# Attention, experts and MLP in one kernel: idle matmuls, a q load and the steps of batches 1 to 3's attention are put elsewhere

## The chip, the cores and the metric

One Trainium2 chip, one of its cores. The metric is the device time of one execution in microseconds (us), as the median of three runs. TensorE is called PE here, VectorE DVE, ScalarE ACT, GpSimd POOL, and SyncE, which issues the loads, SP; those are the profile's own names.

## What is computed

Three stages follow each other. Attention is done twice per batch and head: 32 packed rows `p` attend to `k` and `v`, and then the queries `q` attend to the 32 packed results. Four experts and an MLP work on the result.

```
def sm_attn(qq, kk, vv):
    s = scale * np.matmul(qq, kk.transpose(0, 1, 3, 2))
    a = np.exp(s - np.max(s, axis=-1, keepdims=True))
    a = a / (np.sum(a, axis=-1, keepdims=True) + 1e-09)
    return np.matmul(a, vv)
p_packed = sm_attn(p, k, v)                 # 4 batches, 8 heads, 576 tokens, 64 wide
out = sm_attn(q, p_packed, p_packed)
x = out as 2304 rows of 512
x = sum over 4 experts e of probs[:, e] * (relu(x @ w1[e]) @ w2[e])     # 512 -> 1024 -> 512
r = relu(x @ w_in);  out = (s * r * r + b) @ w_out                      # 512 -> 2048 -> 512
```

## The kernel before

All instructions of one engine run in the order in which the program writes them, and that order is written by hand. Batch 0's attention comes first, as straight code. Then a long loop runs over units: one unit is one expert, one batch, one half of its tokens and one block of 128 hidden columns, 16 units for each expert and batch. In step `i` the loop first runs the pieces that are woven in at that step (`run(i)`, filled by `at(step, function, ...)`), then the first product `m1` of unit `i+2` (6 matmuls of 288 columns, L693), then the second product `m2` of unit `i` (12 matmuls, L721). Each `m1` result goes through ACT (`hh`, L703) and DVE (`hl`, L704). `at_fin` makes the attention result `a2` of a batch, which `m1` of that batch reads. After the last block of a half, DVE takes the four accumulators away into `x2` (L745).

The attention of batches 1 to 3 is woven into these steps, piece by piece. For batch `n` the pieces are numbered from a step `s0`, and a table lists (offset, function, half). The pieces that matter here are, with the names of their tiles:

- `trans_kq`: DVE turns k or q in blocks of 32 (`kT`, `qT`, L148). Two buffers of each half serve both, so the `kT` of the next batch follows on the `qT` of this one.
- `at_s1`: PE multiplies p with k for one half of the tokens (`s1`, 16 matmuls, L187). It needs both `kT` tiles.
- `at_max1`: DVE takes the row maximum (`m2`, L199). For the first half of batches 1 to 3, ACT also copies the scores to SBUF (`a1`, L201), since their PSUM banks are wanted again.
- `at_exp1`: DVE makes the negative maximum `nm` (L208); ACT takes the exponentials of both halves (L219), of the first half from the copy in SBUF, of the second from PSUM.
- `at_a1t`: PE turns the exponentials (`tr`, four matmuls L230 into one bank, one L235 into another), ACT copies them out.
- `at_pv`, `at_pn`, `at_pt`: the product with v (L248), its normalisation by DVE or ACT (`pw`, then `sbd`), and its transposition (L287) with a copy by ACT (`ptw`, L288).
- `at_s2` to `at_fin`: q times the packed rows (L299), softmax over 32 columns on DVE, POOL and ACT (L311 to L339), and `a2` as a high and a low part (L358, L359).

The PSUM banks of tag `m` are two. `s1`, `tr`, `pv`, `pt` and `s2` of batches 1 to 3 and the products `fold_w1` take them in turn, so a matmul that opens a bank waits until whoever read the bank's last content is done. `expert_weights` (L946) is a piece of step 3: four DVE instructions on the gate probabilities and a store.

SP issues the loads in program order, and a load can be issued only when the one eight before it has landed. PE begins with 11 matmuls on a tile of zeros (`warm`, L922), before data is there. Step numbers in the prediction are those of the loop; batch 1 starts at step `s0` = 2, batch 2 at 16, batch 3 at 32.

Of the kernel before, what the change touches and what calls it, by code (L numbers as in the profile page):

```python
# [11 lines left out]
AF = mybir.ActivationFunctionType  # L12
# [7 lines left out]
def attention_experts_mlp_kernel(  # L20
# [87 lines left out]
    def load_k(bi, gi, cuts=None):  # L108
        if ("k", bi, gi) not in kq_in:
            kq_in["k", bi, gi] = att.tile([P, NJ * D], F32, tag="kq", bufs=4, name=f"k{bi}{gi}")  # L110
        x = k_src[bi, 4 * gi : 4 * gi + 4].rearrange("h (r j) d -> (h r) (j d)", j=NJ)
        for c in [slice(None)] if cuts is None else kq_cuts("k", bi)[cuts]:
            nc.sync.dma_start(out=kq_in["k", bi, gi][:, c], in_=x[:, c])
# [17 lines left out]
    def load_v(bi, gi):  # L131
        t = att.tile([P, 4, VC + 1, D], F32, tag="v", bufs=2, name=f"v{bi}{gi}")
        x = v[bi, 4 * gi : 4 * gi + 4]
        nc.sync.dma_start(
            out=t[:, :, :VC, :].rearrange("r h c d -> r h (c d)"),
            in_=x[:, : VC * P, :].rearrange("h (r c) d -> r h (c d)", c=VC),
        )
        nc.sync.dma_start(
            out=t[:VR, :, VC, :], in_=x[:, VC * P :, :].rearrange("h r d -> r h d")
        )  # L140
        v_in[bi, gi] = t
# [58 lines left out]
            if bi and h == 0:  # L200
                nc.scalar.activation(a1[:, :HT], ps, AF.Copy)  # L201

    def at_exp1(bi, c):
        a1, m2 = stt["a1", bi, c]
        nm = att.tile([P, 1], F32, tag="nm", bufs=2, name=f"nm_{bi}{c}")
        s2 = att.tile([P, 2], F32, tag="s2", bufs=2, name=f"s2_{bi}{c}")
        rs = att.tile([P, 1], F32, tag="rs", bufs=2, name=f"rs_{bi}{c}")
        nc.vector.scalar_tensor_tensor(  # L208
            out=nm, in0=m2[:, 0:1], scalar=m2[:, 1:2], in1=nscale, op0=ALU.max, op1=ALU.mult
        )  # L210
        for h in range(2):
            src = stt["s1", bi, h][c][:, :HT]
            dst = a1[:, h * HT : (h + 1) * HT]
            if bi == 0:
                src = src.rearrange("a (r j) -> a r j", r=32)
                dst = a1.rearrange("a (r j) -> a r j", j=NJ)[:, :, blocks((h,))[0]]
            elif h == 0:
                src = dst
            nc.scalar.activation(  # L219
                dst, src, AF.Exp, bias=nm, scale=scale, accum_out=s2[:, h : h + 1]  # L220
            )
        stt["a1", bi, c] = (a1, s2, rs)

    def at_a1t(bi, gi, tags="mm"):
        a1, _, _ = stt["a1", bi, gi]
# [675 lines left out]
    with tc.manual_schedule():  # L901
# [3 lines left out]
        for x in range(2):  # L905
            for gi in range(G):
                load_k(0, gi, slice(x, x + 1))
        load_v(0, 0)
        dp = att.tile([P, NT // P, E], F32, name="dp")
        nc.sync.dma_start(  # L910
# [6 lines left out]
        nc.vector.memset(one, 1.0)  # L917
        nc.vector.memset(least, -896.0)
        make_identity(nc, ident)
        wps = bank("warm", "acc0")  # L920
        for _ in range(WARM):
            nc.tensor.matmul(wps, lhsT=warm[:, :P], rhs=warm, start=True, stop=True)  # L922

        def trans_p(g0, g1):
            nc.vector.transpose(
# [7 lines left out]
        for x in range(2):  # L933
            for gi in range(G):
                trans_kq("k", 0, gi, slice(x, x + 1))
        for c in range(2):
            load_q(0, c)
        for c in range(2):
            load_w1(0, c)
        for f in range(3):  # L940
# [23 lines left out]
        nc.sync.dma_start(out=b_sb, in_=b.partition_broadcast(P))  # L964
        at_s1(0, 0)
        at_s1(0, 1, ("acc0", "acc1"))
        for h in range(2):
            at_max1(0, h)
        at_exp1(0, 0)
        at_a1t(0, 0, ("acc2", "acc3"))  # L970
        at_exp1(0, 1)
# [9 lines left out]
        at_pn(0, 1, act=True)  # L981
        for f in range(2):
            split_w2(0, f)
        at_s2(0, 0, ("acc0", "acc1"))
        for gi in range(G):
            at_pt(0, gi, f"acc{2 + gi}")
# [64 lines left out]
            at(3 + gi, at_a2t, 0, 1, (gi,))  # L1051
            at(4 + gi, at_fin, 0, 1, (gi,), nc.vector)
        for n in range(1, B):
            s0 = (n - 1) * SB + (2 if n == 1 else 0)
            for step, fn, gi in (
                (0, at_s1, 0), (0, at_max1, 0), (1, at_s1, 1), (1, at_max1, 1), (1, at_exp1, 0),
                (1, at_pz, 0), (1, at_pz, 1), (2, at_exp1, 1), (2, at_a1t, 0), (2, at_rs, 0),
                (3, at_pv, 0), (3, at_pn, 0), (4, at_pt, 0), (4, at_a1t, 1), (4, at_rs, 1),
                (5, at_pv, 1), (5, at_pn, 1), (6, at_s2, 0), (6, at_s2t, 0), (6, at_max2, 0),
                (7, at_pt, 1), (7, at_exp2, 0), (8, at_s2, 1), (8, at_s2t, 1), (8, at_max2, 1),  # L1060
                (8, at_norm2, 0), (9, at_a2t, 0), (9, at_exp2, 1), (10, at_norm2, 1),
                (10, at_fin, 0), (11, at_a2t, 1), (12, at_fin, 1),
            ):
                at(s0 + step, fn, n, gi)
            for gi in range(G):
                for x in range(2):
                    at(s0 + 1 + 2 * gi + x, trans_kq, "q", n, gi, slice(x, x + 1))
                if n + 1 < B:
                    at(s0 + 3 + 2 * gi, load_k, n + 1, gi)
                    at(s0 + 6 + gi, load_v, n + 1, gi)  # L1070
                    for x in range(2):
                        at(s0 + 11 + 2 * gi + x, trans_kq, "k", n + 1, gi, slice(x, x + 1))
                    at(s0 + 13 + 2 * gi, load_q, n + 1, gi)
            if n + 1 < B:
                at(s0 + 7, block_p, n + 1)
        for e in range(E):
# [191 lines left out]
```

## Time and profile before

| | |
|---|---|
| runs, median (lowest to highest) | 1124.54 us (1124.49 to 1125.05) |
| the profiled execution: its time, its span | 1126.21 us, 1124.4 us |
| PE busy | 1095.1 us, 97% of the span |
| DVE, ACT, POOL busy | 681.7, 401.1, 287.1 us |
| chain that ended last, by engine | PE 90%, DVE 5%, ACT, POOL, DMA and issue 1% each |

The span is the stretch from the first to the last instruction of the program. A busy PE is one that has a matmul under way, at whichever clock. The granted clock is given as a share of 2.4 GHz: 1.00 is the full clock and 0.50 is 1.2 GHz. Times inside the rows count from the start of the span.

### The profile page before, as it was taken

Reading aid. Unit: us, or ns where it says so; the run is one execution under the profiler, and the core shown is the slowest. Engines: PE = TensorE matmul, PEld = TensorE weight load, DVE = VectorE, ACT = ScalarE, POOL = GpSimd, SP = SyncE. Lnnn points to the kernel's source line nnn. Section 1 sums busy time; section 2 is a strip of 40 time slices with the busy share of each in tenths; the row PEclk is TensorE's granted clock in tenths of the full one; section 3 lists DMA queues with packets and bytes.
Section 4 is the critical chain, followed back from the end, with each engine's and each line's share of the span. In section 5 each row is a group of like instructions: output and inputs, shape, how many; then the busy total and the mean of one; then the engine's idle time right before and its main releaser. Section 6 shows DMA issues by size and latency. Waiting matters only on the chain.

```text
span 1124.4 us, 18679 instructions
## 1 busy us (share of the span) xinstructions
PE 1095.1 (97%) x7275; PEld 1013.3 (90%) x7275; DVE 681.7 (61%) x1249; ACT 401.1 (36%) x786; POOL 287.1 (26%) x337
## 2 busy tenths in 40 slices
PE   8789999999999999999999999999999999999998
PEld 4577888999999899989999999998899999999996
DVE  5767666467657436546446643469945766675554
ACT  3333232364344343333343322345542342342111
POOL 1322111223323144314153352443420120211000
PEclk7899999999999999999999999999999999999999
DMA  9451312013314776766675641345665565655532
GB/s 283 124 155 44 96 30 76 21 52 101 113 40 119 255 241 159 186 219 179 202 232 166 174 133 39 122 168 201 269 254 213 186 206 177 226 196 182 193 113 84
DMA packets 68968, 175.09 MB, mean 156 GB/s; under 512 B 11408, under 2 KB 28048, under 8 KB 68880
## 3 DMA queue, kind: packets, MB, share of 16 engines
q1 hardware_dynamic: 68032, 172.79, 47.8%
q8 instruction: 57, 0.93, 0.3%
q10 hardware_dynamic: 848, 1.11, 0.3%
q14 instruction: 31, 0.25, 0.1%
HBM read 127.44 MB, written 46.44 MB: 155 GB/s over the span
## 4 chain that ended last, share of the span: by engine, by line
PE 90%; DVE 5%; ACT 1%; POOL 1%; issue 1%; DMA 1%; SPq 0%; DVEq 0%; POOLq 0%; ACTq 0%
PE acc L721 35%; PE h L693 18%; PE o L879 17%; PE h L845 15%; PE pp L488 1%; PE pw L389 1%; PE s L299 1%; PE pp L534 1%; PE pv L248 1%; DMA q<-in_q_dram 1%; ACT a L219 1%; PE s L187 1%; DVE kT L148 1%; DVE gg L813 0%; POOL w2l L559 0%
## 5 line engine op out<-in xcount | busy, mean ns | idle before, releaser
L721 PE MATMUL acc<-hh,w2l 128*128 128x288 f32 x1024 | 303.3, 296 | 0.8 <-ACT hh L703 0.6
L721 PE MATMUL acc<-hl,w2h 128*128 128x288 f32 x1024 | 303.4, 296 | 0.0
L721 PE MATMUL acc<-hh,w2h 128*128 128x288 f32 x1024 | 302.9, 296 | 0.0
L693 PE MATMUL h<-a,w1p 128*128 128x288 f32 x1536 | 252.6, 300 | 3.6 <-DVE w1p L404 2.7
L693 PEld LDWEIGHTS h<-a,w1p 128*128 128x128 f32 x1536 | 218.4, 190 | 20.5 <-issue 13.6
L704 DVE SCALAR_TENSOR_TENSOR hl<-h,hh 128x288 fp32r<-128x288 f32 x256 | 116.2, 454 | 190.9 <-ACT hh L703 189.3
L879 PE MATMUL o<-wo,gg 128*128 128x512 f32 x864 | 223.4, 392 | 3.5 <-DVE gg L813 1.9
L845 PE MATMUL h<-xs,wop 128*128 128x384 f32 x1008 | 203.3, 337 | 0.7 <-DVE y L736 0.7
L721 PEld LDWEIGHTS acc<-hh,w2l 128*128 128x128 f32 x1024 | 192.9, 188 | 1.6 <-ACT hh L703 0.8
L721 PEld LDWEIGHTS acc<-hh,w2h 128*128 128x128 f32 x1024 | 193.3, 189 | 0.0
L721 PEld LDWEIGHTS acc<-hl,w2h 128*128 128x128 f32 x1024 | 193.2, 189 | 0.0
L845 PEld LDWEIGHTS h<-xs,wop 128*128 128x128 f32 x1008 | 180.0, 188 | 13.8 <-DVE y L736 1.4
L879 PEld LDWEIGHTS o<-wo,gg 128*128 128x128 f32 x864 | 160.1, 188 | 28.3 <-DVE gg L813 2.8
L703 ACT ACTIVATE hh<-h 128x288 fp32r<-128x288 f32 x256 | 104.3, 408 | 220.4 <-PE h L693 217.4
L747 POOL TENSOR_TENSOR x<-x,y 128x288 f32<-128x288 f32 (+2 forms) x144 | 88.6, 650 | 163.0 <-DVE y L736 162.7
L799 ACT ACTIVATE yy<-yy 128x768 f32<-128x768 f32 x48 | 40.2, 838 | 114.4 <-DVE yy L865 114.4
L865 DVE TENSOR_TENSOR yy<-h,uv 128x384 f32<-128x384 f32 x96 | 51.0, 552 | 46.9 <-PE h L845 46.7
L559 POOL TENSOR_TENSOR w2l<-w2r,w2h 128x512 fp32r<-128x512 f32 x32 | 41.5, 1297 | 85.4 <-ACT w2h L558 83.8
L809 ACT ACTIVATE gg<-yy,b_sb 128x768 fp32r<-128x768 f32 x48 | 44.8, 934 | 37.8 <-DVE yy L802 36.5
L813 DVE SCALAR_TENSOR_TENSOR gg<-yy,b_sb,gg 128x768 fp32r<-128x768 f32 x48 | 55.2, 1149 | 2.4 <-ACT gg L809 2.4
L802 DVE SCALAR_TENSOR_TENSOR yy<-yy,s_sb 128x768 f32<-128x768 f32 x48 | 51.2, 1067 | 0.0
L865 DVE TENSOR_TENSOR uv<-h,uv 128x384 f32<-128x384 f32 x48 | 26.4, 554 | 40.0 <-PE h L845 40.0
(372 smaller groups left out, 1001.0 us busy)
## 6 DMA issues: line engine op xcount, KB each, us to landing
xs<-xs_dram SPq DMA_DIRECT2D x63, 768.0 KB, 4.3
w1p_dram<-w1o SPq DMA_DIRECT2D x32, 512.0 KB, 3.7
w1p<-w1p_dram SPq DMA_DIRECT2D x128, 128.0 KB, 4.4
xs_dram<-xs SPq DMA_DIRECT2D x21, 768.0 KB, 3.3
w2r<-in_moe_w_dram SPq DMA_DIRECT2D x32, 256.0 KB, 4.0
w1r<-in_moe_w_dram SPq DMA_DIRECT2D x12, 512.0 KB, 4.8
q<-in_q_dram SPq DMA_DIRECT2D x16, 288.0 KB, 8.0
pb<-pn_dram SPq DMA_DIRECT2D x16, 288.0 KB, 4.5
```

What stands on the lines that cost most here:

```text
L559: nc.gpsimd.tensor_tensor(out=lo, in0=raw, in1=f32(hi), op=ALU.subtract)
L693: nc.tensor.matmul(t[:, :HT], lhsT=w1p_block(e, bi, f, gi, w), rhs=a2[bi][:, x, gi, tok], start=(n == 0), stop=(n == 3 * G - 1),)
L703: nc.scalar.activation(xh, t[:, :HT], AF.Relu)
L704: nc.vector.scalar_tensor_tensor(out=xl, in0=t[:, :HT], scalar=0.0, in1=f32(xh), op0=ALU.max, op1=ALU.subtract)
L721: nc.tensor.matmul(acc[m][:, :HT], lhsT=w[:, col], rhs=x, start=(f == 0 and n == 0), stop=(f == NF - 1 and n == 2),)
L747: nc.gpsimd.tensor_tensor(out=dst, in0=dst, in1=y[:, a - t0 : z - t0], op=ALU.add)
L802: nc.vector.scalar_tensor_tensor(out=y, in0=y, scalar=s_sb, in1=y, op0=ALU.mult, op1=ALU.mult)
L809: nc.scalar.activation(t[:, 0], y, AF.Identity, bias=b_sb)
L813: nc.vector.scalar_tensor_tensor(out=t[:, 1], in0=y, scalar=b_sb, in1=f32(t[:, 0]), op0=ALU.add, op1=ALU.subtract)
L845: nc.tensor.matmul(ps, lhsT=w[:, a, col], rhs=x[:, z, m, :], start=(n == 0), stop=(n == 3 * HK - 1),)
L865: nc.vector.tensor_tensor(out=dst, in0=ps, in1=src, op=ALU.add)
L879: nc.tensor.matmul(o_acc[i], lhsT=lhsT, rhs=w, start=(f == 0 and n == 0), stop=(f == FG - 1 and n == 2),)
```

## The change

It does six things. It issues the load of batch 0's first q tile before that of v. It takes the two `nm` instructions out of `at_exp1` into a function of their own, `at_nm1`, and lets `at_exp1` do one half at a time. It puts 7 matmuls on the tile of zeros after batch 0's `at_s1`, and 6 before batch 0's first `at_s2`. It lets batch 1's pieces start at step 3 instead of 2, but those of its second half with an offset above 7 stay at their steps. In batches 1 to 3 it makes both `nm` and takes the exponentials of the second half (from PSUM) for both score tiles first, then those of the first half. And it does the `kT` pieces of the next batch, and its q loads, at earlier steps: the `kT` pieces of batch 2 at steps 11 to 14 instead of 13 to 16, those of batch 3 at 26 to 29 instead of 27 to 30.

```diff
+    def at_nm1(bi, c):
...
+        stt["a1", bi, c] = (a1, s2, rs)
+        stt["nm", bi, c] = nm
+
+    def at_exp1(bi, c, hs=(0, 1)):
+        a1, s2, _ = stt["a1", bi, c]
+        for h in hs:
...
+        load_q(0, 0)
         load_v(0, 0)
...
+        def keep_warm(n, tag):
+            wps = bank("warm", tag)
+            for _ in range(n):
+                nc.tensor.matmul(wps, lhsT=warm[:, :P], rhs=warm, start=True, stop=True)
...
-        for c in range(2):
-            load_q(0, c)
+        load_q(0, 1)
...
         at_s1(0, 1, ("acc0", "acc1"))
+        keep_warm(7, "h")
         for h in range(2):
             at_max1(0, h)
+        for c in range(2):
+            at_nm1(0, c)
         at_exp1(0, 0)
...
+        keep_warm(6, "h")
         at_s2(0, 0, ("acc0", "acc1"))
...
-            s0 = (n - 1) * SB + (2 if n == 1 else 0)
-            for step, fn, gi in (
-                (0, at_s1, 0), (0, at_max1, 0), (1, at_s1, 1), (1, at_max1, 1), (1, at_exp1, 0),
-                (1, at_pz, 0), (1, at_pz, 1), (2, at_exp1, 1), (2, at_a1t, 0), (2, at_rs, 0),
+            s0 = (n - 1) * SB + (3 if n == 1 else 0)
+            for step, fn, *args in (
+                (0, at_s1, 0), (0, at_max1, 0), (1, at_s1, 1), (1, at_max1, 1),
+                (1, at_nm1, 0), (1, at_exp1, 0, (1,)), (1, at_nm1, 1), (1, at_exp1, 1, (1,)),
+                (1, at_exp1, 0, (0,)), (1, at_pz, 0), (1, at_pz, 1),
+                (2, at_exp1, 1, (0,)), (2, at_a1t, 0), (2, at_rs, 0),
                 (3, at_pv, 0), (3, at_pn, 0), (4, at_pt, 0), (4, at_a1t, 1), (4, at_rs, 1),
                 (5, at_pv, 1), (5, at_pn, 1), (6, at_s2, 0), (6, at_s2t, 0), (6, at_max2, 0),
                 (7, at_pt, 1), (7, at_exp2, 0), (8, at_s2, 1), (8, at_s2t, 1), (8, at_max2, 1),
...
-                at(s0 + step, fn, n, gi)
+                soon = n == 1 and step > 7 and args[0] == 1
+                at(s0 + step - soon, fn, n, *args)
...
-                        at(s0 + 11 + 2 * gi + x, trans_kq, "k", n + 1, gi, slice(x, x + 1))
-                    at(s0 + 13 + 2 * gi, load_q, n + 1, gi)
+                        at(
+                            (n - 1) * SB + 10 + 2 * gi + x + (n == 1),
+                            trans_kq, "k", n + 1, gi, slice(x, x + 1),
+                        )
+                    at(s0 + 8 + 2 * gi, load_q, n + 1, gi)
```

On DVE, the rows of steps 2 and 3 stand as follows before. `s1_100` and `s1_101` are the scores of batch 1's first half, `hl_0004` belongs to `m1` of unit 4, `ds` and `pn` are `expert_weights`, and `at_010`, `r2_011` belong to batch 0's second softmax.

```order
L148 STREAM_TRANSPOSE kT11_538<-k11_403 128x9x64 x2
L199 TENSOR_REDUCE m2_10_555<-s1_100_545 128x1
L199 TENSOR_REDUCE m2_11_559<-s1_101_546 128x1
L704 SCALAR_TENSOR_TENSOR hl_0004_571<-h_0004_563,hh_0004_570 128x288
L950 TENSOR_REDUCE ds_592<-dp_148 128x18
L951 TENSOR_SCALAR ds_592<-ds_592 128x18
L952 RECIPROCAL ds_592<-ds_592 128x18
L954 TENSOR_TENSOR pn_596<-dp_148,ds_592 128x18x4
L348 STREAM_TRANSPOSE at_010_601<-sc_01_348 128x288
```

The same place on DVE now:

```order
L148 STREAM_TRANSPOSE kT11_553<-k11_418 128x9x64 x2
L709 SCALAR_TENSOR_TENSOR hl_0004_568<-h_0004_560,hh_0004_567 128x288
L959 TENSOR_REDUCE ds_589<-dp_151 128x18
L960 TENSOR_SCALAR ds_589<-ds_589 128x18
L961 RECIPROCAL ds_589<-ds_589 128x18
L963 TENSOR_TENSOR pn_593<-dp_151,ds_589 128x18x4
L353 STREAM_TRANSPOSE at_010_598<-sc_01_363 128x288
L341 TENSOR_REDUCE r2_011_600<-sc_01_363 128x9
L342 TENSOR_SCALAR r2_011_600<-r2_011_600 128x9
L343 RECIPROCAL r2_011_600<-r2_011_600 128x9
L199 TENSOR_REDUCE m2_10_615<-s1_100_605 128x1
L199 TENSOR_REDUCE m2_11_619<-s1_101_606 128x1
```

The two maxima of batch 1 have moved behind `expert_weights` and a part of batch 0's softmax.

On ACT, the rows around batch 2's exponentials (step 17 and the start of step 18) stand as follows before; `a1_20` and `a1_21` are the two tiles of exponentials, `s1_210` and `s1_211` the scores of the second half in PSUM.

```order
L703 ACTIVATE hh_0102_1180<-h_0102_1173 128x288
L219 ACTIVATE a1_20_1166,s2_20_1216<-a1_20_1166,nm_20_1215 128x288
L219 ACTIVATE a1_20_1166,s2_20_1216<-s1_210_1203,nm_20_1215 128x288
L703 ACTIVATE hh_0103_1236<-h_0103_1229 128x288
L219 ACTIVATE a1_21_1170,s2_21_1253<-a1_21_1170,nm_21_1252 128x288
L219 ACTIVATE a1_21_1170,s2_21_1253<-s1_211_1204,nm_21_1252 128x288
```

The same place on ACT now:

```order
L708 ACTIVATE hh_0102_1198<-h_0102_1191 128x288
L224 ACTIVATE a1_20_1184,s2_20_1231<-s1_210_1218,nm_20_1230 128x288
L224 ACTIVATE a1_21_1188,s2_21_1236<-s1_211_1219,nm_21_1235 128x288
L224 ACTIVATE a1_20_1184,s2_20_1231<-a1_20_1184,nm_20_1230 128x288
L708 ACTIVATE hh_0103_1256<-h_0103_1249 128x288
L224 ACTIVATE a1_21_1188,s2_21_1236<-a1_21_1188,nm_21_1235 128x288
```

Three exponentials now stand ahead of `hh_0103` instead of two, and the second one of them is the one that reads `s1_211`.

On DVE at the change from step 15 to 16, before; `acc_0012` and `acc_0013` are accumulators that DVE takes away, `kT21` is the second `kT` tile of batch 2, and `s1_200` its first scores.

```order
L745 TENSOR_TENSOR x2_0_842<-acc_0013_882,pb_00_599 128x96
L745 TENSOR_TENSOR x2_1_1146<-acc_0013_882,pb_00_599 128x192
L148 STREAM_TRANSPOSE kT21_1104<-k21_817 128x9x64
L199 TENSOR_REDUCE m2_20_1165<-s1_200_1155 128x1
L199 TENSOR_REDUCE m2_21_1169<-s1_201_1156 128x1
```

The same engine now, from the last `kT21` on:

```order
L148 STREAM_TRANSPOSE kT21_1071<-k21_860 128x9x64
L709 SCALAR_TENSOR_TENSOR hl_0100_1110<-h_0100_1102,hh_0100_1109 128x288
L409 TENSOR_TENSOR w1p_012_1130<-pw1_012_1125,w1p_012_1130 128x512
L409 TENSOR_TENSOR w1p_013_1138<-pw1_013_1133,w1p_013_1138 128x512
L709 SCALAR_TENSOR_TENSOR hl_0101_1149<-h_0101_1141,hh_0101_1148 128x288
L750 TENSOR_TENSOR x2_0_839<-acc_0010_875,pb_00_596 128x96
```

The last transposition of `kT21` has moved from behind the eight `x2` rows to a place two steps ahead of them.

## Rows read from the trace of the kernel before

**Rows 1.** Waits of PE, whole span: total, times, longest (us).

```profile
PE tr L235 <- ACT a L219: 6.1, 3, 3.4
PE s L187 <- DVE kT L148: 4.7, 2, 3.0
```

**Rows 2.** Issues of SP around 9 us: start, length (us).

```profile
8.93 0.47 SPq L119 DMA_DIRECT2D q<-in_q_dram  x1
```

**Rows 3.** DMA issues of 8.8 to 9.3 us: size, us to landing.

```profile
q<-in_q_dram SPq DMA_DIRECT2D x1, 288.0 KB, 8.1
```

**Rows 4.** Chain that ended last, first 26 us: start, length (us).

```profile
6.43 8.01 DMA q<-in_q_dram
...
17.17 2.34 DVE qT L148
...
21.32 3.43 PE s L299 x16
```

**Rows 5.** Timeline of PE, first 29 us: start, length, [idle before, releaser].

```profile
1.45 4.58 PE L922 MATMUL warm<-warm 128*128 128x512 f32 x11 [1.45 <-DVE least L918]
...
12.26 1.13 PE L230 MATMUL tr<-ident,a 128*128 128x128 f32 x4 [2.20 <-ACT a L219]
...
26.75 1.20 PE L299 MATMUL s<-qT,sbd 64*64 64x288 f32 x16
```

**Rows 6.** Stretches: PE busy (matmuls), granted clock, DMA share, GB/s.

```profile
12.16:25.82 13.66, 12.28 (x70) 0.50 1.08 303
...
46.30:49.71 3.41, 3.41 (x20) 0.50 0.00 0
...
59.95:63.37 3.42, 3.35 (x15) 0.50 0.42 174
...
100.00:104.00 4.00, 2.29 (x22) 1.00 0.00 0
```

**Rows 7.** Timeline of PE, DVE and POOL, 45 to 61 us.

```profile
45.99 1.92 PE L187 MATMUL s<-kT,pbd 64*64 64x288 f32 x12 [3.04 <-DVE kT L148]
...
55.86 0.74 PE L230 MATMUL tr<-ident,a 128*128 128x128 f32 x4 [0.81 <-ACT a L219]
60.02 0.42 PE L235 MATMUL tr<-ident,a 128*64 128x128 f32 x1 [3.42 <-ACT a L219]
...
50.56 0.22 DVE L950 TENSOR_REDUCE ds<-dp 128x18 f32<-128x72 f32 x1
50.81 1.24 DVE L951 TENSOR_SCALAR ds<-ds 128x18 f32<-128x18 f32 x1
...
53.72 0.76 DVE L199 TENSOR_REDUCE m<-s 128x1 f32<-128x288 f32 x2
...
56.99 1.29 DVE L359 TENSOR_TENSOR a<-at,a 128x288 fp32r<-128x288 f32 x1 [0.39 <-ACT a L358]
...
50.75 1.27 POOL L559 TENSOR_TENSOR w2l<-w2r,w2h 128x512 fp32r<-128x512 f32 x1 [6.26 <-ACT w2h L558]
```

**Rows 8.** One line over the whole span: ns shortest, median, longest.

```profile
L337 DVE TENSOR_SCALAR r<-r x10: 172/176/1254, 28.0 to 194.6; 128x18 f32<-128x18 f32 x6, 128x9 f32<-128x9 f32 x4
```

**Rows 9.** Chain that ended last, one step of the loop at 200 us.

```profile
199.98 0.80 PE h L693 x6
200.78 1.59 PE acc L721 x12
```

**Rows 10.** Timeline of PE and ACT, 101 to 114 us (batch 2).

```profile
103.69 1.19 PE L187 MATMUL s<-kT,pbd 64*64 64x288 f32 x12 [1.71 <-DVE kT L148]
...
112.98 0.30 PE L235 MATMUL tr<-ident,a 128*64 128x128 f32 x1 [1.34 <-ACT a L219]
...
109.70 0.54 ACT L219 ACTIVATE a<-a,nm 128x288 f32<-128x288 f32 x1 [3.23 <-DVE nm L208]
```

**Rows 11.** Timeline of ACT and POOL, 79 and 92 us (batch 1).

```profile
79.17 0.28 ACT L288 ACTIVATE ptw<-pt 128x128 f32<-128x128 f32 x1 [1.28 <-PE pt L287]
...
92.05 1.44 POOL L359 TENSOR_TENSOR a<-at,a 128x576 fp32r<-128x576 f32 x1
```

More of the change, by code (lines that the diff above doesn't have):

```diff
@@ L201, in at_max1 @@
                 nc.scalar.activation(a1[:, :HT], ps, AF.Copy)
-    def at_exp1(bi, c):
+    def at_nm1(bi, c):
         a1, m2 = stt["a1", bi, c]
@@ L210, in at_exp1 @@
         )
-        for h in range(2):
+        stt["a1", bi, c] = (a1, s2, rs)
[3 more added lines that the diff above has]
+        for h in hs:
             src = stt["s1", bi, h][c][:, :HT]
@@ L219, in at_exp1 @@
             nc.scalar.activation(
-                dst, src, AF.Exp, bias=nm, scale=scale, accum_out=s2[:, h : h + 1]
+                dst, src, AF.Exp,
+                bias=stt["nm", bi, c], scale=scale, accum_out=s2[:, h : h + 1],
             )
-        stt["a1", bi, c] = (a1, s2, rs)
     def at_a1t(bi, gi, tags="mm"):
@@ L919, in attention_experts_mlp_kernel @@
         make_identity(nc, ident)
-        wps = bank("warm", "acc0")
-        for _ in range(WARM):
-            nc.tensor.matmul(wps, lhsT=warm[:, :P], rhs=warm, start=True, stop=True)
+        def keep_warm(n, tag):
+            wps = bank("warm", tag)
+            for _ in range(n):
+                nc.tensor.matmul(wps, lhsT=warm[:, :P], rhs=warm, start=True, stop=True)
+        keep_warm(WARM, "acc0")
         def trans_p(g0, g1):
```

## The prediction

> **What bounds the kernel now.** I read the busy shares first: PE is busy 97% of the span, so nothing is to be had but what PE waits, and what it does at half clock. The list of PE's waits puts most of the waiting into two lines: `tr` L235 for ACT's exponentials, 6.1 us in three waits, and `s1` L187 for DVE's `kT`, 4.7 us in two [rows 1]. The timeline places them: 3.04, 0.81 and 3.42 us in batch 1's attention between 42 and 60 us [rows 7], 1.71 and 1.34 us in batch 2's [rows 10], and the rest of the 6.1, 6.1 - 3.42 - 1.34 = 1.3 us, in batch 3's. The reader is to see next, in the stretches, that PE worked at 0.50 of its clock from 12.16 to 25.82, from 46.30 to 49.71 and from 59.95 to 63.37 [rows 6]. The last two stretches come right behind the waits of 3.04 and 3.42 us. In the 26 us ahead of that, the chain of what ended last runs over the q load, DVE's transposition of it, and `s2` [rows 4].
>
> **The early part.** The q load first. Both q tiles are wanted: DVE transposes the second from 17.17 on [rows 4]. Its last piece was issued at 8.93 and took 8.1 us [rows 2, 3], so it landed at 17.03, just ahead of that. The change lets the first tile land sooner, but the second keeps the same bytes ahead of it (k, both v, the first q), so I leave it at 17.03 and count 0. The most that it could bring is that the second tile lands when the first does now, 6.43 + 8.01 = 14.44 [rows 4]: 2.6 us. Now v lands later, about when the first q did, 14.4, where PE starts `pv` at 14.08 by its timeline; these 0.3 us lie ahead of the same DVE work and cost nothing.
>
> So `s2` cannot start before 21.3, as now [rows 4]. What can shrink is its own 3.43 us, which were at half clock; the same 16 matmuls took 1.20 us at full clock [rows 5]. Half of them also wait for `pw` and `sbd` of the second half, which come sooner if `pv` is faster. With the full clock throughout, `s2` would end some 1.9 us earlier (21.3, plus 0.3 for the second `sbd`, plus 1.2). The 7 idle matmuls fill the gap of 2.20 us ahead of `tr` [rows 5], after which the clock fell. But `tr` and `pv` alone did not raise it again in 9 us [rows 6], so I take it that it falls behind them. Then the 6 idle matmuls stand in PE's queue ahead of `s2`: 11 took 4.58 us at the start [rows 5], so 6 at half clock cost 2.5 us, from about 20.7 to 23.2. That is the worst end: `s2` follows at half clock and ends 0.9 us late. In between, they raise the clock while they run, as the first eleven did, and `s2` ends near 24.0 instead of 24.7. I take **+0.7**, with ends of -0.9 and +1.9 (+2.6 more if the second q came early). The DVE chain behind `s2` up to the first `m1` is unchanged and moves as it stands.
>
> **Batch 1's attention, steps 2 to 5.** Removed are the waits 3.04 + 0.81 + 3.42 = 7.3 us [rows 7], and the two stretches at half clock, 6.8 us long with work that takes half of that, 3.4 us: 10.7 us. New waits, in the old times: `m1` and `m2` of a step, 0.80 + 1.59 = 2.4 us [rows 9], now come ahead of `s1`, from 42.25 (where `s1` started before, by the timeline) to 44.65. `s1` does its first four matmuls and waits for the last `kT11`, 45.99 as before: 0.8 us. It ends at 46.9, the next step's pair at 49.3. The second `s1` needs the banks that the first one filled, so it waits for DVE's maxima and ACT's copies. These stand behind `expert_weights` now, as the order shows. DVE: 45.99, plus 0.46 for `hl`, plus the block from 50.56 to 53.72 [rows 7]. In that block, L951 took 1.24 us for 18 columns a partition, and it ended just after POOL's `w2l` (50.75 + 1.27 = 52.02) [rows 7]; a like instruction, L337, takes 0.17 us at its shortest and 1.25 at its longest [rows 8]. In the new order POOL's `w2l` of that step is done by about 45.7, before L951 starts at 46.7, so I take 0.17 for it: the block takes 3.16 - 1.07 = 2.1 us, and the two maxima 0.76: 49.3. The first copy then is done near 49.7, so the wait is 0.4 us; with the long L951 it would be 1.5.
>
> The page "SBUF — State Buffer" of the Trainium skill (section "Who interferes with whom") gives a reason: DVE and POOL share one pair of SBUF ports, one instruction holds it to its end, and who starts first blocks the other. By that rule too the new order frees L951; by row L951 alone the sum below would be 1.1 us smaller, and the longest L337 agrees with the rule, as it ended with a `w2l` in the timeline.
>
> Then `tr`: the second `s1` (1.2) and the pair (2.4) leave PE free at 53.3. DVE in the meantime has `hl` behind ACT's copies (to 51.1), L359's subtraction, which I leave at 1.29 since POOL's `w2l` again runs beside it [rows 7], a transposition of 0.4, two maxima and two `nm` of 0.2 each: near 54.2. Three exponentials at 0.53 apiece (the first at 109.70 [rows 10], the next at 110.23 in the timeline) end at 55.8: `tr` waits 2.4 us. But its second bank is free by then, so L235 doesn't wait again. Net: 10.7 - 0.8 - 0.4 - 2.4 = **+7.1**, with ends of +5 (long L951, half a us of other lateness) and +8.4 (the three waits at half).
>
> **Batch 1's tail.** `pt` and the second `s2` now are woven into one step, 10, without a pair between them. The second bank of `s2` is that of `pt`, which ACT's copy of 0.28 us [rows 11] must have read, with a start and an end of the same order: **-0.45**, between 0 and -1.
>
> **Batch 2's `kT`.** Its last transposition stood behind eight `x2` rows on DVE and kept `s1` waiting 1.71 us [rows 10]; two steps sooner it is done before PE comes: **+1.7**. Of batch 3's, no wait is listed [rows 1], so its one step counts 0. The q loads at earlier steps go out on an SP queue that nothing waits for there; they cost nothing, as the DMA engines are nearly idle then (a share near 0 from 100 to 104 [rows 6]), and POOL's, PE's and DVE's rows are the same in number.
>
> **The exponentials of batches 2 and 3.** L235 waited 1.34 and 1.3 us because its bank still was to be read by the fourth exponential. Now that is the second. But the first `tr` needs the third: 109.70 + 3 x 0.53 = 111.3, where PE stood ready at 111.0 (112.98 less the wait of 1.34 and less 0.63 for four transpositions by the timeline). So a new wait of 0.35 each: 2.64 - 0.7 = **+1.9**, between +1.5 and +2.3. `hh` of that step comes 0.5 us later, with a step of 2.4 us to spare.
>
> **The sum.** 0.7 + 7.1 - 0.45 + 1.7 + 1.9 = 11.0 us. The profiled execution took 1126.21 us with a span of 1124.4, 1.7 above the median of 1124.54; 11.0 less than its own time is 1115.2, and off the median **1113.5**.
>
> **The rivals.**
> - *The clock falls in the new wait of 2.4 us.* Idle times of 2.20, 3.04 and 3.42 us were each followed by a stretch at half clock [rows 5 to 7], one of 1.71 was not [rows 6, 10]. A stretch of 3.4 us costs 1.7: 1115.2. I give 0.22, since the wait lies just over the shortest that lost it.
> - *The clock holds through batch 0's products.* Then +1.9 in place of +0.7: 1112.3, and less if the second q lands early too. 0.18.
> - *Batch 1 comes too late for the experts.* `a2` of its first half is due at `m1` of unit 16 in step 14; POOL's part ended at 92.05 + 1.44 = 93.49 [rows 11], and that `m1` began at 94.35 by the timeline, 0.9 us to spare. Its pieces move a step later, with `kT` rows ahead of them on DVE. But POOL's row stood behind one of the second half, which is not moved, so I expect 0.4 us to spare still. If it slips the whole step, PE waits 2.4 - 0.9 = 1.5 us: 1115.0. 0.06.
> - *DVE, not PE, sets the pace of 42 to 60 us.* Then moving `s1` only moves the waits, and 3.9 us remain (0.7 - 0.45 + 1.7 + 1.9): 1120.7. For it speaks that DVE was without a break from 35 to 46 us in the timeline, against it that PE then has 2.4 us of other work to put there. 0.07.
> - *The change does not do what it says*: the idle matmuls hold no clock, q gains nothing, and new waits eat the rest to within 2.2 us. 0.04.
> - *Slower: the half clock stays.* PE's bursts around the new waits could be too thin to raise it between 26 and 60 us. Those 34 us hold 6.8 at half clock now and some 7 of waiting; of the other 20 each us at half clock costs one more. The point where it decides is 11 us of them: then the gain is gone, and with all 20 the time is 1133. Against it: all stretches from 46 us on ended with PE at work [rows 6]. 0.03.
>
> **How the numbers follow.** The sum as it stands has 0.40, the forecast. A measurement of this kernel can tell about 0.2%, 2.2 us, from no change: the first five cases (0.40 + 0.22 + 0.18 + 0.06 + 0.07) are faster by more, 0.93; the same 0.04; slower 0.03. The ends of the terms taken together give 1110.1 (1.9 + 8.4 + 0 + 1.7 + 2.3 = 14.3) and 1118.2 (-0.9 + 5 - 1 + 1.7 + 1.5 = 6.3). Eight in ten lie between 1110.5 and 1117.5: that leaves out the last three rivals (0.14) and the outermost ends.
>
> **What would show it.** The second q transposition should start at 17.2 again, and `s2` end between 22.8 and 24.2. The waits of PE should list `s1` for `kT11` once, under 1 us, `s1` for ACT's copies, new and under 0.6, and `tr` L230 with about 2.4 us in batch 1 and 0.35 in the two others; L235 should be gone. L951 should take 0.17. Behind batch 1's start, at most one stretch at half clock. I am wrong if DVE's maxima of batch 1 come later than 49.5 (old times), if the clock stays low around `tr`, or if unit 16's `m1` waits for `a2`.

## The result, and the profile after

| | before | after |
|---|---|---|
| median (lowest to highest), same chip | 1124.51 us (1124.35 to 1125.05), 4 runs | 1111.67 us (1109.32 to 1112.94), 4 runs |
| the profiled execution: its time, its span | 1126.21, 1124.4 us | 1111.21, 1109.4 us |

The ratio is 0.9883 (95% interval 0.9865 to 0.99): 12.8 us, 1.2%, are gone, where 11.0 were forecast. 1113.5 was predicted, with 1110.5 to 1117.5 around it. Between the two profiled executions it is 15.0 us, because that of before lay 1.7 above its median and that of after 0.5 below. The list of PE's waits answers to [rows 1]:

```profile
PE h L698 <- DVE w1p L409: 2.8, 1, 2.8
PE tr L235 <- ACT a L224: 2.2, 4, 1.4
PE o L884 <- DVE gg L818: 1.9, 1, 1.9
PE s L187 <- DVE kT L148: 0.7, 1, 0.7
```

L235 is now the line of the first four transpositions. Before, that was L230, whose waits [rows 1] does not list:

```profile
PE tr L230 <- ACT a L219: 3.0, 2, 2.2
```

So the 6.1 us of the fifth transposition (L240 now) are gone, the 3.0 us of the first four have become 2.2, and the 4.7 us for `kT` have become 0.7. The stretches, as in [rows 6], each with its length, then the busy time of PE, PEld (PE's loads of weights), DVE, ACT and POOL with the number of instructions, the granted clock, the DMA share and GB/s:

```profile
7.16:31.05 23.89, 18.42 (x157) 11.33 (x155) 17.99 (x40) 9.44 (x27) 3.54 (x4) 1.00 1.05 294
31.05:34.47 3.42, 3.42 (x16) 1.99 (x15) 2.52 (x6) 1.01 (x2) 0.62 (x3) 0.50 1.04 299
34.47:747.85 713.38, 707.37 (x5355) 675.55 (x5355) 418.92 (x844) 265.89 (x560) 232.97 (x282) 1.00 0.44 134
747.85:751.26 3.41, 3.41 (x12) 3.02 (x11) 3.41 (x4) 0.94 (x1) 2.02 (x1) 0.50 0.41 171
```

The clock never falls between 7 and 31 us, and batch 1's two half-clock stretches are gone. The early part on PE, as in [rows 5]:

```profile
9.96 1.89 PE L930 MATMUL warm<-warm 128*128 128x512 f32 x7
12.24 0.74 PE L235 MATMUL tr<-ident,a 128*128 128x128 f32 x4 [0.40 <-ACT a L224]
...
17.70 1.65 PE L930 MATMUL warm<-warm 128*128 128x512 f32 x6
20.55 1.54 PE L304 MATMUL s<-qT,sbd 64*64 64x288 f32 x16 [1.19 <-DVE sbd L286]
...
29.44 1.79 PE L698 MATMUL h<-a,w1p 128*128 128x288 f32 x11 [2.81 <-DVE w1p L409]
```

`s2` takes 1.54 us instead of 3.43 [rows 4]. The chain has the second q tile landing at 8.27 + 8.13 = 16.40, where it was 17.08, and DVE's transposition behind it, against [rows 4]:

```profile
8.27 8.13 DMA q<-in_q_dram
...
16.50 2.34 DVE qT L148
```

Batch 1, as in [rows 7], on PE, DVE, POOL and ACT:

```profile
43.75 1.19 PE L187 MATMUL s<-kT,pbd 64*64 64x288 f32 x12 [0.66 <-DVE kT L148]
52.63 0.74 PE L235 MATMUL tr<-ident,a 128*128 128x128 f32 x4 [1.35 <-ACT a L224]
...
44.14 0.18 DVE L960 TENSOR_SCALAR ds<-ds 128x18 f32<-128x18 f32 x1
45.98 0.76 DVE L199 TENSOR_REDUCE m<-s 128x1 f32<-128x288 f32 x2
48.37 1.31 DVE L364 TENSOR_TENSOR a<-at,a 128x288 fp32r<-128x288 f32 x1 [0.39 <-ACT a L363]
50.00 0.78 DVE L199 TENSOR_REDUCE m<-s 128x1 f32<-128x288 f32 x2
...
48.08 1.28 POOL L564 TENSOR_TENSOR w2l<-w2r,w2h 128x512 fp32r<-128x512 f32 x1 [1.26 <-ACT w2h L563]
...
50.99 0.50 ACT L224 ACTIVATE a<-s,nm 128x288 f32<-128x288 f32 x1 [2.66 <-DVE nm L208]
51.96 0.53 ACT L224 ACTIVATE a<-a,nm 128x288 f32<-128x288 f32 x1
```

L960, which was L951, takes 0.18 us where no `w2l` lies beside it; L364, beside one, still takes 1.31.

To place the gain, I compare the start of the same row in both timelines. The first `m1` starts 2.23 us sooner (31.67, now 29.44). DVE's `hl` of unit 16, the first of batch 1, is 10.26 sooner (95.84, now 85.58). That of unit 20, behind batch 2's waits, is 13.74 sooner (114.55, now 100.81), and that of unit 36, in batch 2's experts and behind batch 3's attention, 14.83 (168.56, now 153.73). So of the 15.0 us between these two executions the early part brought 2.23, batch 1 8.03, batch 2 3.48, batch 3 1.09 and the rest of the span 0.2.

### The profile page after: what moved, and what is told of

Its sections match the earlier page's. It is cut to its first block, busy times and chain, and to the rows that moved or that the text cites. A ratio compares the mean times of both kernels' runs of the same rounds, so it can differ in the third digit from the quotient of the medians.

```text
span 1109.4 us, 18704 instructions
## 1 busy us (share of the span) xinstructions
PE 1091.2 (98%) x7288; PEld 1012.4 (91%) x7288; DVE 679.6 (61%) x1249; ACT 401.0 (36%) x786; POOL 286.9 (26%) x337
## 4 chain that ended last, share of the span: by engine, by line
PE 92%; DVE 4%; DMA 1%; POOL 1%; issue 1%; ACT 1%; SPq 0%; DVEq 0%; POOLq 0%; ACTq 0%
PE acc L726 35%; PE h L698 18%; PE o L884 17%; PE h L850 15%; PE pp L493 1%; PE pw L394 1%; DMA q<-in_q_dram 1%; PE pp L539 1%; PE s L304 1%; PE pv L253 1%; DVE gg L818 0%; POOL w2l L564 0%; POOL x L752 0%; PE s L187 0%; DVE yy L807 0%
## 5 line engine op out<-in xcount | busy, mean ns | idle before, releaser
L675 POOL TENSOR_TENSOR wo<-wo 128x512 fp32r<-128x512 f32 x16 | 24.0, 1506 | 103.2 <-ACT wo L674 103.2
```

## The experiments

The ratios are to the kernel before on the same chip, where its median was 1125.5 to 1126.1 us. Each experiment left one trace; with those of before and after there are 14. The changed kernel has two of these, every other kernel one.

**The changed kernel once more.** No edit.

> The changed kernel as it is, once more, beside the others on one chip. Theory (the stretch at half clock at 748 us, behind a wait of 1.87 us, comes in some executions and not in others, and so does the time at which the second q tile lands): the first m1 starts 8.9 us after s2 again and the waits of batches 1 to 3 repeat within 0.1 us, while the stretch near 748 us may be missing and q may land up to 1 us elsewhere; ratio to the kernel before 0.987 to 0.990. Rival (these are of the program): the stretch at 748 and the second q transposition at 16.5 repeat.

Measured: 1110.74 us, 0.9871 (0.9857 to 0.9884). `m1` came 8.89 us after `s2`, the waits were 0.67 and 1.40 again. The stretch at 748 us was missing, and q landed at 16.68. So that stretch comes in some executions and not in others. The wait of 1.9 us for `gg` ahead of it stands in all 14 traces, and half clock followed in 6 of them.

**Without the idle matmuls.**

```diff
-        keep_warm(7, "h")
...
-        keep_warm(6, "h")
```

> The changed kernel without its 7 and 6 idle matmuls, all else as changed. Theory (the idle matmuls hold the clock): the wait of some 2.2 us ahead of the first transposition of batch 0's exponentials is empty again, the clock goes to 0.50 behind it, and s2 takes about 3.4 us again instead of 1.54. The second q tile still comes 0.7 us sooner than in the kernel before, so DVE takes the first s2 bank near 24.1 (before 24.74, changed 22.12), and the first m1 starts near 31.0 (31.67, 29.44): 1.6 us lost, 1113.3. Rival (the clock holds because q comes sooner, not because of the idle matmuls): first m1 within 0.3 us of 29.44, and 1111.7. Second rival (the 6 stand in the way of s2): first m1 near 28.9, 1111.2.

Measured: 1113.42 us, 0.9895 (0.9881 to 0.991). PE's timeline:

```profile
12.24 1.03 PE L235 MATMUL tr<-ident,a 128*128 128x128 f32 x4 [2.21 <-ACT a L224]
...
30.47 0.82 PE L698 MATMUL h<-a,w1p 128*128 128x288 f32 x2 [2.81 <-DVE w1p L409]
```

Its stretches:

```profile
12.50:19.32 6.82, 6.35 (x44) 4.52 (x45) 3.83 (x8) 2.46 (x8) 0.00 (x0) 0.50 1.05 285
...
29.57:36.39 6.82, 5.92 (x23) 4.54 (x24) 4.33 (x10) 2.56 (x6) 1.41 (x4) 0.50 0.96 243
```

The wait of 2.21 us and the half clock behind it are back, so in the changed kernel the idle matmuls hold the clock there. All 14 traces agree: in the three without idle matmuls the clock fell between 12.2 and 12.5 us and stayed low for 6.8 to 17.1 us; in the 11 with them it did not fall there, and in three of these it fell later, still ahead of the wait of the first `m1` (at 17.39, 22.55 and 24.43), each time for 3.41 us. But here the clock rose again at 19.32, with PE on transpositions and `pv`, so `s2` ran at full clock and did not take the 3.4 us that I had expected. The first `m1` came 1.03 us later, and the half clock around it lasted 6.82 us instead of 3.42: `kT11` was done 15.3 us after `m1` instead of 14.2. At `hl` of unit 16 2.11 us were lost (87.69 against 85.58), so about half of the loss lies in the longer stretch. Whether that belongs to the edit is not shown. By the ratios the loss is 1.4 or 2.7 us against the two measurements of the changed kernel, on other chips; the intervals overlap, so its size is not settled.

**The idle matmuls alone, and with the early q load, in the kernel before.**

```diff
+        load_q(0, 0)                 # second kernel only
         load_v(0, 0)
...
-        for c in range(2):           # second kernel only
-            load_q(0, c)
+        load_q(0, 1)
...
+        keep_warm(7, "h")
...
+        keep_warm(6, "h")
```

> The kernel before with the 7 and 6 idle matmuls and nothing else of the change. Theory (they hold the clock by themselves): granted clock 1.00 from the start to 30 us, s2 takes 1.54 instead of 3.4 us, the first m1 starts 8.9 us after the start of s2 (before 10.35, changed 8.89) and 1.4 us sooner than before; the waits and half-clock stretches of batch 1 stay: 1.4 us below the kernel before. Rival (the early q load is needed for it as well): 0.50 from 12 or 16 us on, the first m1 10 us or more after s2, 0 to 0.5 us gained or lost.

> The kernel before with the idle matmuls and the early load of the first q tile, and nothing of the later steps changed. Theory (the two work together: the idle matmuls save something only where the second q tile is there before the clock falls behind the wait for it, and the first tile sooner makes that likelier): first m1 9.0 us after the start of s2, granted clock 1.00 to 29 us or more, 1.5 to 2.3 us below the kernel before, ratio 0.998 to 0.9987. Rival (only q's landing decides, and it scatters by more than the order moves it): 0 to 0.5 us, ratio 0.9995 or more, as with the idle matmuls alone. Second rival (what the early part gains is given back in batch 1's waits for kT11, which DVE sets): the first m1 sooner by 1.5 us or more, but the wait of s1 longer by the same, and the first x2 row at the old distance.

Measured: 1125.78 us, 1.0006 (0.9995 to 1.0017) for the idle matmuls alone, and 1126.09 us, 1.0001 (0.9992 to 1.001) with the q load: nothing from either. In the first, q landed at 18.45, PE waited 3.0 us for `sbd` and the clock fell at 22.55 after all. In the second the clock held to 31.9. Its PE timeline:

```profile
22.89 1.55 PE L299 MATMUL s<-qT,sbd 64*64 64x288 f32 x16 [1.45 <-DVE sbd L281]
...
31.80 3.14 PE L693 MATMUL h<-a,w1p 128*128 128x288 f32 x12 [2.81 <-DVE w1p L404]
46.00 2.19 PE L187 MATMUL s<-kT,pbd 64*64 64x288 f32 x12 [3.06 <-DVE kT L148]
60.31 0.42 PE L235 MATMUL tr<-ident,a 128*64 128x128 f32 x1 [3.41 <-ACT a L219]
```

`m1` follows `s2` by 8.91 us, as with the whole change (before 10.35). But q landed at 18.74, 1.66 later than in the trace of before, and batch 1's two stretches at half clock lasted 6.83 us each instead of 3.41. The times fit the first rival, by which q's landing decides. But the mean granted clock of the 12 runs was 0.989 to 0.995, against 0.987 to 0.991 before, and the time did not follow it. In the one trace, what was gained behind `s2` was lost to the late q and the longer stretches. What took it back in the runs without a trace stays open.

**The q order undone**, in the changed kernel.

```diff
-        load_q(0, 0)
         load_v(0, 0)
...
-        load_q(0, 1)
+        for c in range(2):
+            load_q(0, c)
```

> The changed kernel with both q tiles of batch 0 loaded where they were, behind v. Theory (the 0.68 us by which the second q transposition started sooner came from the order of the loads): that transposition starts at 17.1 to 17.2 again instead of 16.50, s2 and the first m1 come 0.7 us later (first m1 near 30.1), the clock stays at 1.00 through batch 0's products: 1112.4. Rival (it came from the clock or from chance in the landing): the transposition starts near 16.5 all the same, 1111.7. Second rival (without the early q tile the clock falls in spite of the idle matmuls, since DVE and PE come in other gaps): a half-clock stretch from about 12 on, first m1 near 31.7, 1113.9.

Measured: 1112.62 us, 0.9889 (0.9876 to 0.9902). The second q landed at 17.64, `m1` started at 30.90, the clock held. It looks like the theory, but the landings of all traces say more. In the new order (9 traces) the second q landed between 16.38 and 18.93, 17.65 on average; in the old order (5 traces) between 17.08 and 19.45, 18.40 on average. The difference of 0.75 us is smaller than the scatter of either, so these traces do not show that the order brings anything. In all 14, `s2` started 4.1 to 4.4 us after that landing.

**Batch 1 at its old step.**

```diff
-            s0 = (n - 1) * SB + (3 if n == 1 else 0)
+            s0 = (n - 1) * SB + (2 if n == 1 else 0)
...
-                soon = n == 1 and step > 7 and args[0] == 1
+                soon = 0
```

> The changed kernel with batch 1's pieces at step 2 again, and those of its second half with them. Theory (one step later removes the waits of batch 1): s1 waits for the last kT11 about 3 us again, and the transposition of the exponentials waits for ACT, in total 6 us or more between 40 and 60 us, against 0.66 + 1.35 in the changed kernel; where a wait is over 2 us a stretch at half clock follows, one or two of 1.7 us each. 4 us of waits and 1.7 to 3.4 us of clock: 1117.4 to 1119.1. Rival (DVE sets the pace of 42 to 60 us, so that the waits only move): under 2 us lost, at most 1113.7.

Measured: 1116.25 us, 0.9922 (0.9909 to 0.9935). PE's timeline in batch 1:

```profile
46.12 2.18 PE L187 MATMUL s<-kT,pbd 64*64 64x288 f32 x12 [3.18 <-DVE kT L148]
56.74 0.75 PE L235 MATMUL tr<-ident,a 128*128 128x128 f32 x4 [0.35 <-ACT a L224]
```

The stretch behind the first of these waits:

```profile
45.38:52.20 6.82, 6.08 (x28) 4.74 (x29) 3.09 (x6) 1.70 (x4) 1.06 (x1) 0.50 0.11 32
```

The wait for `kT11` and the half clock are back, that for ACT is not: the new order of the exponentials shortens it at either step. From the first `m1` to `hl` of unit 20, 75.09 - 71.37 = 3.7 us were lost, and by the ratios 4.4 or 5.7 against the two measurements of the changed kernel. The rival with DVE as the pace allowed 2.

**The old order of the exponentials**, in the changed kernel, and **the new order alone**, in the kernel before (the reverse of this diff, and `at_nm1` split off).

```diff
-                (1, at_nm1, 0), (1, at_exp1, 0, (1,)), (1, at_nm1, 1), (1, at_exp1, 1, (1,)),
-                (1, at_exp1, 0, (0,)), (1, at_pz, 0), (1, at_pz, 1),
-                (2, at_exp1, 1, (0,)), (2, at_a1t, 0), (2, at_rs, 0),
+                (1, at_nm1, 0), (1, at_exp1, 0), (1, at_pz, 0), (1, at_pz, 1),
+                (2, at_nm1, 1), (2, at_exp1, 1), (2, at_a1t, 0), (2, at_rs, 0),
```

> The changed kernel with the exponentials in the old order: for each score tile the first half (from SBUF) and then the second (from PSUM). Theory (the second bank of the transposed exponentials waits for the fourth exponential only when that is the one that reads the bank): the waits of L235's successor are back at about 1.3 us each in batches 2 and 3, and in batch 1 the second bank waits for the fourth exponential, behind one more hh on ACT, 1 to 1.5 us; the waits of 0.24, 0.18 and 1.35 for the first bank shrink by up to 0.2 each. 1.1 + 1.1 + 1.2 = 3.4 us lost: 1115.1. Rival (only batches 2 and 3 gain, batch 1's wait is the same either way): 2.2 us, 1113.9. Second rival (the order counts for nothing, the waits were those of the late kT): within 0.5 us of 1111.7.

> The kernel before with the new order of the exponentials and nothing else of the change. Theory (the order alone removes the waits for the fourth exponential, in batch 1 too): of the 6.1 us of these waits nothing is left, the stretch at half clock behind the longest (3.42 us) goes with it, and new waits for the third exponential of 0.2 to 0.4 us come in each batch: 6.1 + 1.7 - 0.9 = 6.9 us below the kernel before, ratio 0.9939. This is what undoing it in the changed kernel cost. Rival (in batch 1 the order helps only together with the step's shift, since the scores of the second half come late there): 2.2 us, ratio 0.998.

Measured: undone 1118.76 us, 0.9939 (0.9925 to 0.9953); alone 1119.71 us, 0.994 (0.9927 to 0.9954). It is the largest part by itself: some 6.5 us alone, and undone 6.3 or 7.7 by the ratios against the two measurements of the changed kernel. Undone, the fifth transposition waits in each of the three batches, 5.7 us in all, and longest in batch 1, as PE's timeline shows:

```profile
53.53 0.75 PE L235 MATMUL tr<-ident,a 128*128 128x128 f32 x4 [0.88 <-ACT a L224]
57.33 0.42 PE L240 MATMUL tr<-ident,a 128*64 128x128 f32 x1 [3.06 <-ACT a L224]
```

The clock fell in that wait:

```profile
55.27:62.09 6.82, 4.76 (x21) 4.48 (x23) 2.65 (x6) 2.79 (x8) 1.65 (x2) 0.50 0.13 51
```

I had expected 1.2 us of wait there and no stretch, and 1115.1 us. Two of the six runs came near that: they took 1115.79 and 1115.93 us at a mean granted clock of 0.998, and the other four 1118.47 to 1120.41 at 0.994 or 0.995. A mean of 0.998 over 1114 us leaves at most 5.6 us at half clock, so in those two the stretch of 6.82 us was missing or shorter. They lie 4 to 5 us above the medians of the changed kernel. Alone, the order meets the old wait for `kT11` (3.27 us), and L240 does not wait; so it needs no help from the step's shift.

**The old steps of `kT`** (batch 2's at 13 to 16 again) and of the q loads that follow on them, in the changed kernel.

```diff
-                            (n - 1) * SB + 10 + 2 * gi + x + (n == 1),
+                            (n - 1) * SB + 11 + 2 * gi + x + 2 * (n == 1),
...
-                    at(s0 + 8 + 2 * gi, load_q, n + 1, gi)
+                    at((n - 1) * SB + 13 + 2 * gi + 2 * (n == 1), load_q, n + 1, gi)
```

> The changed kernel with the kT pieces and q loads at their old steps (batch 2's at steps 13 to 16). Theory (the last kT of batch 2 stands behind eight x2 rows and PE waits for it): a wait of s1 for kT of 1.7 us near 93 us, no fall of the clock behind it, nothing else: 1.7 us above the changed kernel on the same chip. Rival (batch 1's shift by a step has moved that wait away by itself): no such wait, no loss.

Measured: 1114.59 us, 0.9903 (0.9889 to 0.9916), 3.9 above the changed kernel on the same chip. PE's first `s1` of batch 2 and an earlier wait, and `hl` of units 16 and 20 on DVE:

```profile
16.34 0.87 PE L253 MATMUL pv<-v,a1t 128*64 128x128 f32 x10 [1.29 <-DMA v<-in_v_dram]
...
92.28 0.70 PE L187 MATMUL s<-kT,pbd 64*64 64x288 f32 x4
94.69 1.19 PE L187 MATMUL s<-kT,pbd 64*64 64x288 f32 x12 [1.71 <-DVE kT L148]
...
86.85 0.46 DVE L709 SCALAR_TENSOR_TENSOR hl<-h,hh 128x288 fp32r<-128x288 f32 x1 [0.22 <-ACT hh L708]
104.48 0.46 DVE L709 SCALAR_TENSOR_TENSOR hl<-h,hh 128x288 fp32r<-128x288 f32 x1
```

The wait is the one of [rows 10], 1.71 us. But between the two `hl` lie 17.63 us, and in the changed kernel 100.81 - 85.58 = 15.23: the late `kT` costs 2.4 us, 0.7 more than the listed wait. The difference builds up within the 16 matmuls of `s1`, at full clock: four and twelve of them, split by the wait, take 0.70 and 1.19 us, where in the changed kernel all 16 take 1.20 in one go.

```profile
91.01 1.20 PE L187 MATMUL s<-kT,pbd 64*64 64x288 f32 x16
```

In this trace another 1.27 us lie ahead of that (86.85 - 85.58), where the edit changes nothing: q landed at 18.93, `pv` waited 1.29 us for v, and the clock was at 0.50 from 17.39 to 20.80. No half clock followed on the first `m1` here.

**Idle matmuls ahead of the first `m1`**, in the changed kernel.

```diff
         fold_hi(0, 0, 1)
+        keep_warm(10, "h")
```

> The changed kernel with 10 more idle matmuls ahead of the first m1, which fill most of the wait of 2.8 us for the folded weights (26.6 to 29.4 us). Theory (the half clock from 31.05 to 34.47 comes from that wait): the stretch is gone, the work in it takes half of 3.4 us: 1.7 us gained, with m1 at most 0.2 us later. Rival (it comes from the gaps behind m1, where PE waits for hh and hl): the stretch stays, 0 gained. Second rival (the idle matmuls end late and hold m1 up): 0 to 0.5 lost.

Measured: 1111.04 us, 0.9874 (0.9856 to 0.9893); the four runs were 1108.83 to 1112.86. On PE:

```profile
27.58 2.56 PE L930 MATMUL warm<-warm 128*128 128x512 f32 x10
30.46 1.91 PE L698 MATMUL h<-a,w1p 128*128 128x288 f32 x12 [0.32 <-DVE w1p L409]
```

The clock was 1.00 from 6.31 us to the end. The stretch behind the first `m1` is missing in all three traces with these matmuls and stands in 9 of the 11 without them, so it comes from the wait of 2.8 us (1.7 in one of the two exceptions), though not always. From `m1` to the last `kT11` it is 12.95 us instead of 14.2, 1.25 gained. The medians do not show it. The four runs differ in their clock: the two at a mean of 1.000 took 1108.83 and 1109.82 us, those at 0.998 and 0.995 took 1112.26 and 1112.86.

**A version meant to be faster**: those 10, 10 instead of 6 ahead of `s2`, and two low parts of `a2` on POOL; and the same with both q tiles behind v.

```diff
-        keep_warm(6, "h")
+        keep_warm(10, "h")
...
+        keep_warm(10, "h")           # ahead of the first m1
...
-            at(4 + gi, at_fin, 0, 1, (gi,), nc.vector)
+            at(4 + gi, at_fin, 0, 1, (gi,))
```

> The changed kernel with 10 idle matmuls ahead of the first m1, 10 instead of 6 ahead of the first s2, and the low part of batch 0's second a2 on POOL instead of DVE (two instructions of 1.31 us that ran beside POOL's w2l). Theory: DVE comes 0.9 to 1.3 us sooner to the maxima of step 4, so the wait of the transposition for ACT falls from 1.35 to 0.5 us or less; no half clock from 29 to 35 us, 1.3 us; the idle matmuls lie in waits of 1.2 and 2.8 us and hold nothing up: 2.1 us below the changed kernel, ratio 0.985 to 0.986. Rival (DVE sets the pace of 30 to 60 us): s1 waits for kT11 longer by what the rest gains, and the ratio stays at 0.987. Second rival (POOL is late with the low part): m1 of unit 8 waits, ratio 0.987 or more.

> The same as the one above it, but with both q tiles of batch 0 loaded behind v, as in the kernel before. Theory (the second q tile has the same bytes ahead of it, so the order gives nothing): within 0.5 us of the one above, and no wait of pv for v. Rival (the new order lands the second q tile 0.7 us sooner, as the traces of before and after show it): 0.7 us or more above. Second rival (the new order costs, as pv then waits for v by 0.8 and 1.3 us in two of the runs so far): 0.5 us or more below.

Measured: 1110.66 us, 0.987 (0.9852 to 0.9889), and 1110.88 us, 0.9864 (0.9851 to 0.9877). Neither is told from the changed kernel, nor one from the other, though the second q landed at 17.92 in the first and at 19.39 in the second. The forecast was 0.985 to 0.986, and the ratio is the one of the rival that DVE sets the pace. But in the trace of the first, 54.10 us lie between the first `m1` and `hl` of unit 16 (30.97 to 85.07), where in the changed kernel there are 56.14: 2.0 us are gained there, while the first `m1` came 1.53 later with its q. Whether the landing also hid the gain in the other runs is not shown. In the second, PE waited 2.73 us for `sbd`, and the clock fell from 24.43 to 27.84. PE, DVE and POOL of the first:

```profile
52.12 0.75 PE L235 MATMUL tr<-ident,a 128*128 128x128 f32 x4 [0.60 <-ACT a L224]
...
48.95 0.82 DVE L199 TENSOR_REDUCE m<-s 128x1 f32<-128x288 f32 x2 [0.36 <-PE s L187]
49.69 0.82 DVE L208 SCALAR_TENSOR_TENSOR nm<-m,nscale 128x1 f32<-128x1 f32 x2
...
49.55 0.81 POOL L364 TENSOR_TENSOR a<-at,a 128x288 fp32r<-128x288 f32 x1
```

The wait of 1.35 us fell to 0.60: DVE without its L364 reaches the maxima early enough to wait for PE. With the idle matmuls ahead of `m1` alone it was 1.42, so it is L364, stretched beside `w2l`, that makes up 0.75 of the 1.35 us. The first `nm` now lies beside POOL's L364, and the two `nm` take 0.82 us instead of 0.33.

## Why the prediction was right, and where its steps were off

The time was right and so was the mechanism of the largest term. The sizes were off: between the two traces every stage gave more than forecast, 15.0 us in all against 11.0. Of these, 2.2 are the distance of the two executions from their medians, so the medians, 12.8 apart, lie nearer to the forecast than the terms do; that part of the agreement is luck. (The sum of the favourable ends, 14.3 us off 1124.54, is 1110.2 and not 1110.1.)

**The early part, +0.7.** The step that failed is "so I take it that it falls behind them". The clock held through `tr`, `pv` and `s2`, here and in 8 of the 11 traces with idle matmuls; that was the second rival (1112.3), and nearer to the result than the forecast. From `s2` to `m1` it saved 10.35 - 8.89 = 1.46 us, and `s2` started 0.77 sooner. The latter is q's landing, counted at 0; whether the order or chance brought it can't be told. The two early edits alone moved no median. Taking the idle matmuls out of the changed kernel cost 1.4 or 2.7 us by the ratios, which is not clear of their intervals.

**Batch 1, +7.1.** 8.03 were measured, tail included. The wait for `kT11` was 0.66 (0.8 foreseen), L951's successor took 0.18 (0.17), the wait for ACT's copies was absent (0.4). `tr` waited 1.35 instead of 2.4, since ACT's copies, and `hh` and `hl` behind them, began behind the first of the two maxima instead of behind both: DVE was through with the second maxima at 50.78, and ACT's third exponential ended at 52.49, some 1.1 us sooner than worked out, in the old times. No half clock followed, so the first rival did not come; waits of 1.35 to 1.42 us in the same place left the clock alone in the other traces too. What the term did not say is which edit carries it: the order of the exponentials, of which I counted 1.9 us in batches 2 and 3, is worth 6 to 8 by the two experiments, since batch 1's wait of 3.42 us and the half clock behind it [rows 6, 7] go with the order, at either step. The step carries the wait for `kT11` and the half clock behind that. Undone one at a time, the order, the step, the `kT` steps and the idle matmuls cost 7.0, 5.1, 2.9 and 2.0 us by the ratios, against the mean of the changed kernel's two (0.9877). That is 17 us, more than the whole change brought, so these prices do not add up.

**The tail, -0.45.** It cost nothing: PE was busy throughout.

```profile
61.90:90.70 28.80, 28.80 (x237) 24.52 (x236) 20.92 (x43) 8.41 (x17) 9.17 (x13) 1.00 0.46 124
118.70:171.50 52.80, 52.67 (x438) 46.25 (x437) 33.97 (x75) 15.97 (x40) 7.84 (x9) 1.00 0.21 59
```

The first row holds unit 16's `m1` as well, so the rival of a late `a2` did not come either.

**Batch 2's `kT`, +1.7.** Right as a mechanism; it measured 2.4, since the stall slows the `s1` around it.

**The exponentials of batches 2 and 3, +1.9.** The waits of 1.34 and 1.30 us are gone, and the new ones are 0.18 in batch 2 and none in batch 3 (second row above), where I expected 0.35 each: about 2.2, which is what batches 2 and 3 brought beyond the 2.4 (3.48 - 2.4 + 1.09).

The slower rival and that of the change doing nothing are out by the ratio; "DVE sets the pace" by the step experiment and by the wait for `kT11` of 0.66 us.

## What to carry to other kernels

A bank is free when its last reader is done, so what reads PSUM goes ahead of what reads SBUF. In this kernel four instructions of each batch in another order brought by themselves some 6.5 us, half of the gain. A listed wait is a lower bound of its price where the clock falls behind it, or where the work around it slows down, so compare the times of one and the same later row. An early saving is worth measuring alone and with the rest: here it brought nothing alone, and perhaps 1 to 3 us with the later waits gone. And a single trace has its own luck: compare the mean granted clock of all runs before a stretch at half clock is counted as the kernel's.

## What the runs showed of the hardware that I had not expected

- **The clock.** PE's waits of 3.0 us and more were followed by half clock in every trace (though in two runs of the old order of the exponentials the stretch was missing or shorter), those of 1.35 to 1.42 us for the exponentials of batch 1 in none. In between it differed: the wait of 1.71 us for `kT21` was followed by it in one of five traces, that of 1.9 for `gg` in 6 of 14, and that of 2.7 to 2.8 ahead of the first `m1` in all but one of ten. A wait of 2.23 us for `sbd` was not followed by it; that of 2.2 ahead of the first `tr` was, in three of three. And length is not all: behind the 1.29 us for v, with the old `kT` steps, the clock fell, and behind 1.78 us for `sbd`, at batch 1's old step, it did not. At the other end, with `pv` and transpositions at half clock ahead, it had risen by 19.32 in one trace, where it stayed low to 25.82 in [rows 6] and to 29.45 with the new order alone. The page "TensorE: Matmul & The Clock Gate" of the Trainium skill (Part 1) calls the number of slow matmuls at a start run-variable. These traces agree: the 11 idle matmuls at the start took from 4.17 to 5.06 us. They show the same of a fall in mid-kernel.
- **DVE beside POOL.** A subtraction of 288 columns took 1.31 us on DVE beside POOL's `w2l` and 0.81 on POOL; beside it there, the two `nm` on DVE took 0.82 instead of 0.33. In the changed kernel this subtraction ended 0.3 us behind POOL's `w2l`, and L951 before ended 0.03 us behind it [rows 7]. The page "SBUF — State Buffer" (section "Who interferes with whom") of the Trainium skill has two SBUF inputs on DVE contend with a POOL instruction that reads SBUF; the rows of the subtraction and of `nm` agree.
- **Landings.** The same q load, behind the same loads on its queue, landed up to 2.5 us apart between the traces, and `s2` follows it. That is as much as most edits here are worth. These are traces of different kernels; the two of the changed kernel have it at 16.40 and 16.68. How much of the scatter comes from the kernel and how much from the execution is not shown.
